# Spreading attention's reciprocals over features by DMA instead of by matmul, with a new order of the work around it

## The chip, the cores and the metric

The kernel runs on one core of one Trainium2 chip. The metric is device time in microseconds (us) of one execution. The kernel before took 1003.21 us (median of 4 runs, 1002.76 to 1003.95).

## The reference, cut to what matters

Linear attention over 8 batches of 8 heads (576 tokens, 64 features) is followed by a mixture of 8 experts. Only the attention's last division is concerned here:

```python
num = np.einsum('bhsf,bhfd->bhsd', q_p, kv)
den = np.einsum('bhsf,bhf->bhs', q_p, z)[..., None] + 1e-06
return (num / den).astype(np.float32)
```

There is one denominator for each head and token, and each divides 64 features. The expert layer after it takes the result with features on partitions, so every reciprocal must be present on the 64 partitions of its head.

## The kernel before

From about 24 to 184 us the kernel runs seven blocks, 0 to 6. Block j does the feed-forward of expert 0 for 512 tokens in 16 slots: slots 0 to 7 are the first matrix (`ffn1`), slots 8 to 15 the second (`ffn2`). The attention of batch b = j + 1 is scattered over these slots. Instructions keep the written order on TensorE (PE), VectorE (DVE) and ScalarE (ACT). The loads go through GpSimd's queue (POOL), the others through SyncE's (SP).

The reciprocals are split into two fp16 parts and spread over partitions by matmuls with a matrix of zeros and ones; ScalarE copies the result from PSUM, and VectorE multiplies:

```python
def attend(b, hk):
    parts = ((0, 2 * C3), (2 * C3, C))
    rb_ps = [ps_s.tile([P, 512], FP32, name="small_ps") for _ in parts]
    rb = rb_pool.tile([P, C * HP], FP32, name="rb")
    for i, (c0, c1) in enumerate(parts):
        for j in range(c0 // C3, c1 // C3):
            te.matmul(out=rb_ps[i][...], lhsT=spread[0:96, j, hk]..., rhs=hls[b][:], ...)
        se.copy(out=rb[:, c0 * HP : c1 * HP], in_=rb_ps[i][...])
    num_ps = [ps_s.tile([P, 512], FP32, name="small_ps") for _ in parts]
    for i, (c0, c1) in enumerate(parts):
        for hh in range(2):
            te.matmul(out=num_ps[i][...], lhsT=kvs[b][0][:, hk, hh, :], rhs=qTs[b, hk][...], ...)
        ve.tensor_tensor(out=xT[:, hk, ...], in0=num_ps[i][...], in1=rb[...], op=ALU.mult)

# schedule of a block j with batch b = j + 1 (cut)
at(j, 5, denominators, b)
for hk in range(HK):
    at(j, FT + 2 * hk, attend, b, hk)          # slots 8, 10, 12, 14
for half in range(2):
    at(j, 2 * half if j else 3, load, b + 1, half)
```

`small_ps` is a pool of four PSUM buffers. A half load is three DMAs (k, v and q of four heads), each 288 KB as written.

The softmax here doesn't subtract the row's maximum and nothing guards it: scores larger than these inputs give would overflow.

## Time and profile before

| what | number | where it is read |
|---|---|---|
| span of the profiled run | 1000.8 us | head of the page |
| one block, blocks 2 to 5 | 22.2 to 22.3 us | start of `ffn1` to start of the next, timeline of PE |
| PE busy in such a block | 21.9 to 22.0 us | windows |
| three spread matmuls | 0.34 us | timeline of PE |

The windows view of the kernel before, one line for each of blocks 2 to 5. The columns are the stretch, its length, the busy us and instruction count of each engine, the granted clock of PE, the DMA share and GB/s.

```profile
73.37:95.56 22.19, 21.87 (x244) 11.66 (x241) 17.33 (x37) 14.34 (x33) 4.30 (x6) 1.00 0.57 82
95.56:117.85 22.29, 21.97 (x247) 11.76 (x245) 17.33 (x37) 14.34 (x33) 4.29 (x6) 1.00 0.58 81
117.85:140.04 22.19, 21.87 (x243) 11.67 (x241) 17.34 (x37) 14.34 (x33) 2.15 (x3) 1.00 0.46 68
140.04:162.33 22.29, 21.97 (x247) 11.78 (x245) 17.34 (x37) 14.34 (x33) 0.00 (x0) 1.00 0.01 2
```

PE is idle for 0.3 us a block, the other engines for 4.9 us and more. Time can be saved only by taking work or waits from PE. The timeline of PE in the kernel before shows both (start, us, what; the bracket is the idle time before it and what ended it):

```profile
86.30 0.41 PE L100 MATMUL small_ps<-hl,acc_hi 96*128 96x192 f16 x3
86.64 0.44 PE L100 MATMUL small_ps<-q_pT,kv_sb 128*64 128x384 f16 x4
...
100.25 0.50 PE L100 MATMUL small_ps<-ident,q_p 128*128 128x128 f16 x6 [0.26 <-ACT kv_sb L100]
```

The three spread matmuls of one attend hold PE from 86.30 to 86.64. Four attends make 1.36 us a batch.

### The profile page before, as it was taken

The numbers are of one execution on the slowest core, as the hardware profiler recorded it, in microseconds if no ns is written. First come the engines' busy times: TensorE is split into PE (matmuls) and PEld (weight loads), VectorE is DVE, ScalarE is ACT, GpSimd is POOL, SyncE is SP. The second block draws the span as 40 slices with busy tenths as digits, with TensorE's granted clock in tenths as the row PEclk, the third lists the DMA queues.
The fourth block names the chain that finished last, engine by engine and source line by source line (L and its number), as shares of the span: only waits on it lengthen the run. The fifth ranks groups of instructions, "written<-read, shape, count | busy, mean of one in ns | idle before, by whom it ended". The sixth has DMA issues, their size and how long they took to land.

```text
span 1000.8 us, 20629 instructions
## 1 busy us (share of the span) xinstructions
PE 981.3 (98%) x8062; PEld 689.3 (69%) x8062; DVE 829.2 (83%) x1862; ACT 574.7 (57%) x1284; POOL 60.3 (6%) x82
## 2 busy tenths in 40 slices
PE   7999999989999999999999999999999999999997
PEld 6455555446777777777777777777777777777775
DVE  5888777588989888888879878988789888988886
ACT  5766666447777555555555555555555555555551
POOL 6412200001000000000000000000000000000001
PEclk9999999999999999999999999999999999999999
DMA  9966610534002331034013320043113400104535
GB/s 165 206 92 87 87 23 1 105 70 82 33 25 51 65 66 48 26 76 80 25 48 67 60 55 26 25 90 66 41 33 67 90 25 25 48 25 111 130 89 124
DMA packets 51922, 66.50 MB, mean 66 GB/s; under 512 B 4848, under 2 KB 43760, under 8 KB 51824
## 3 DMA queue, kind: packets, MB, share of 16 engines
q0 software_dynamic: 27232, 30.94, 20.0%
q1 hardware_dynamic: 24352, 33.98, 12.4%
q8 instruction: 63, 1.03, 0.4%
q10 hardware_dynamic: 240, 0.26, 0.1%
q14 instruction: 35, 0.29, 0.1%
HBM read 83.12 MB, written 12.98 MB: 96 GB/s over the span
## 4 chain that ended last, share of the span: by engine, by line
PE 72%; issue 21%; DVE 4%; ACT 1%; DMA 1%; POOL 1%; POOLq 0%; ACTq 0%; DVEq 0%
PE rows_ps L100 25%; PE h_ps L100 21%; PE copied_ps L100 8%; PE p_ps L100 8%; PE y_ps L100 5%; PE small_ps L100 5%; DVE k_p L100 1%; DMA v_ld<-in_v_dram 1%; DVE q_pT L100 1%; DVE q_p L100 0%; DVE den L100 0%; DVE xT L100 0%; DVE acc_lo L100 0%; DVE P_tok L100 0%; DVE v_aug_240 L100 0%
## 5 line engine op out<-in xcount | busy, mean ns | idle before, releaser
L762 DVE SCALAR_TENSOR_TENSOR acc_lo<-rows_ps,P_tok,acc_lo 128x512 f32<-128x512 f32 (+1 forms) x322 | 203.1, 639 | 74.8 <-PE rows_ps L100 74.7
L100 PEld LDWEIGHTS <-H 128*128 128x128 f16 x2080 | 203.0, 98 | 83.1 <-issue 1.2
L100 PEld LDWEIGHTS <-w1e 128*128 128x128 f16 x1632 | 155.9, 98 | 59.2 <-issue 4.9
L100 PE MATMUL h_ps<-xT,w1e 128*128 128x384 f16 (+1 forms) x616 | 152.9, 350 | 0.0
L730 ACT ACTIVATE H<-h_ps 128x384 f16<-128x384 f32 x144 | 70.6, 490 | 95.1 <-PE h_ps L100 95.1
L100 PE MATMUL rows_ps<-w2e,H 128*128 128x256 f16 (+1 forms) x568 | 91.2, 285 | 0.0
L711 ACT COPY copied_ps<-h_ps 128x384 f32<-128x384 f32 x144 | 67.5, 469 | 35.3 <-PE h_ps L100 35.3
L721 ACT ACTIVATE H<-copied_ps 128x384 f16<-128x384 f32 x144 | 70.8, 492 | 20.4 <-PE copied_ps L100 20.4
L100 PE MATMUL copied_ps<-xT,w1e 128*128 128x384 f16 x336 | 82.1, 326 | 0.0
L100 PE MATMUL copied_ps<-w2e,H 128*128 128x256 f16 x504 | 75.6, 272 | 0.0
L762 DVE SCALAR_TENSOR_TENSOR acc_lo<-copied_ps,P_tok,acc_lo 128x256 f32<-128x256 f32 x126 | 60.0, 476 | 0.6 <-PE copied_ps L100 0.2
L762 DVE SCALAR_TENSOR_TENSOR acc_hi<-rows_ps,P_tok,acc_hi 128x512 f32<-128x512 f32 (+1 forms) x56 | 41.3, 737 | 20.4 <-PE rows_ps L100 19.6
L777 DVE TENSOR_TENSOR H<-H 128x512 f16<-128x512 f16 x125 | 52.6, 421 | 2.6
L100 PE MATMUL y_ps<-w2e,hT 128*128 128x512 f16 x224 | 54.7, 380 | 0.0
L804 ACT COPY copied_ps<-rows_ps 128x256 f32<-128x256 f32 x111 | 39.7, 357 | 17.6 <-PE rows_ps L100 17.6
L100 ACT ACTIVATE hT<-h_ps 128x512 f16<-128x512 f32 x54 | 32.3, 600 | 17.0 <-PE h_ps L100 16.6
L100 DVE TENSOR_TENSOR xT<-small_ps,rb 128x384 f16<-128x384 f32 x64 | 26.2, 451 | 16.6 <-ACT rb L100 16.5
L118 POOL DMA_DIRECT2D w1e<-in_moe_w_dram x11 | 8.3, 763 | 509.0 <-DVE T_3_5030 L670 92.4
L100 PEld LDWEIGHTS <-hT 128*128 128x128 f16 x224 | 19.5, 98 | 25.0 <-issue 5.8
L100 ACT COPY rb<-small_ps 128x384 f32<-128x384 f32 x64 | 22.4, 402 | 22.7 <-PE small_ps L100 22.6
L100 DVE TENSOR_SCALAR q_pT<-small_ps 128x384 f16<-128x384 f32 x46 | 25.0, 552 | 9.3 <-PE small_ps L100 8.7
L100 ACT ACTIVATE H<-h_ps 128x384 f16<-128x384 f32 (+1 forms) x40 | 21.3, 532 | 15.4 <-PE h_ps L100 14.7
(2459 smaller groups left out, 2065.8 us busy)
## 6 DMA issues: line engine op xcount, KB each, us to landing
out_dram<-acc_lo SPq DMA_DIRECT2D x62, 128.0 KB, 2.4
w1e<-in_moe_w_dram POOLq DMA_DIRECT2D x7, 1024.0 KB, 8.9
w2e<-in_moe_w_dram POOLq DMA_DIRECT2D x7, 1024.0 KB, 9.5
k_ld<-in_k_dram POOLq DMA_DIRECT2D x16, 288.0 KB, 6.4
v_ld<-in_v_dram POOLq DMA_DIRECT2D x16, 288.0 KB, 7.3
q_ld<-in_q_dram POOLq DMA_DIRECT2D x16, 288.0 KB, 6.8
w1e<-in_moe_w_dram POOLq DMA_DIRECT2D x4, 256.0 KB, 10.4
w2e<-in_moe_w_dram POOLq DMA_DIRECT2D x4, 256.0 KB, 10.9
```

Source lines behind the costliest of these rows:

```text
L100: i = getattr(self.engine, name)(*args, **kwargs)
L118: nc.gpsimd.dma_start(out=w[0][:, :, f0:f1], in_=view[:, :, f0:f1])
L711: se.copy(out=Y[:, 0:TU], in_=X[:, 0:TU])
L721: se.activation(out=h11, in_=Y[:, 0:TU], func=AF.Relu)
L730: se.activation(out=h12, in_=X[:, 0:TU], func=AF.Relu)
L762: ve.scalar_tensor_tensor(out=a, in0=rows, scalar=P_tok[:, g, self.e : self.e + 1], in1=a, op0=ALU.mult, op1=ALU.add,)
L777: i = (nc.gpsimd if self.last else ve).tensor_tensor(out=out_, in0=in0, in1=in1, op=op)
L804: se.copy(out=self.W, in_=self.U)
```

## The change

For batches 3 to 7 the reciprocals go to DRAM in one store and come back in eight reads, each of which repeats rows over 64 partitions. Spread matmuls and PSUM copies of these batches go. To give the DMAs time, the denominators move to slot 4 (from block 3 on; block 2 keeps slot 5), the attends to slots 12 to 15, and much of the next batch's work comes a block earlier. Turns (transposes of q) come one a slot and more of them on ScalarE; y copies go to ScalarE. The loads are written in slots 13 and 15, behind the reads. `v_augs` moves into a part of the accumulator that is not in use yet, to make room for four `rb` buffers.

```diff
-            if g % 2 == 0:
+            if g % 2 == 0 or TCH // P <= g < (B - 1) * TCH // P:
                 se.copy(out=acc(g), in_=y_ps)
@@ denominators
             ve.reciprocal(out=den[:], in_=den[:])
+            if b >= 3:
+                r = dram.tile([96, C3 * HP], FP32, name="r")
+                nc.sync.dma_start(out=r[:], in_=den[:])
+                for hk in range(HK):
+                    rb = rb_pool.tile([P, C * HP], FP32, name="rb")
+                    for hh in range(2):
+                        h = 2 * hk + hh
+                        nc.sync.dma_start(
+                            out=rb[hh * HP : (hh + 1) * HP, :].rearrange("p (j s) -> p j s", j=3),
+                            in_=r[:].rearrange("(j r) s -> r j s", r=32)[h : h + 1].to_broadcast(
+                                [HP, 3, C3 * HP]
+                            ),
+                        )
+                    rbs[b, hk] = rb
+                return
@@ schedule (cut)
-                at(j, 5, denominators, b)
+                at(j, 5 if j <= 2 else 4, denominators, b)
                 for hk in range(HK):
-                    at(j, FT + 2 * hk, attend, b, hk)
+                    at(j, 8 + 2 * hk if j == 1 else 12 + hk, attend, b, hk)
...
+                for i, (hk, k_) in enumerate(turns[:8]):
+                    at(j, 8 + i, turn, b + 1, hk, k_, k_ != 1)
+                at(j, 10, sums, b + 1, 0)
+            if 1 <= j and b + 2 < B:
+                for half in range(2):
+                    at(j, 13 + 2 * half, load, b + 2, half)
```

More of the change, by code (lines that the diff above doesn't have):

```diff
@@ L179 @@
         kv_pool = p1.enter_context(tc.tile_pool(name="kv_pool", bufs=2))
-        rb_pool = p1.enter_context(tc.tile_pool(name="rb_pool", bufs=2))
+        rb_pool = p1.enter_context(tc.tile_pool(name="rb_pool", bufs=4))
         ps_y = p1.enter_context(tc.tile_pool(name="ps_y", bufs=2, space=bass.MemoryType.PSUM))
@@ L287 @@
         ve.tensor_copy(out=wg[:], in_=wg_ld[:])
-        kps, qps, qTs, kvs, hls = {}, {}, {}, {}, {}
-        v_augs = [cs_pool.tile([P, C, D + 2], F16, name=f"v_aug{i}") for i in range(4)]
+        kps, qps, qTs, kvs, hls, rbs = {}, {}, {}, {}, {}, {}
+        lent = acc_lo[:, G_LO - 4 : G_LO, :].rearrange("p g d -> p (g d)").bitcast(F16)
+        VA = C * (D + 2)
+        v_augs = [
+            lent[:, i * VA : (i + 1) * VA].rearrange("p (c d) -> p c d", d=D + 2)
+            for i in range(4)
+        ]
         for t in v_augs:
@@ L396, in denominators @@
             ve.reciprocal(out=den[:], in_=den[:])
+            if b >= 3:
[6 more added lines that the diff above has]
+                        nc.sync.dma_start(
+                            out=rb[hh * HP : (hh + 1) * HP, :].rearrange(
+                                "p (j s) -> p j s", j=3
+                            ),
+                            in_=r[:].rearrange("(j r) s -> r j s", r=32)[h : h + 1].to_broadcast(
+                                [HP, 3, C3 * HP]
+                            ),
+                        )
+                    rbs[b, hk] = rb
+                return
             hi = kv_pool.tile([96, C3 * HP], F16, name="hi")
@@ L408, in attend @@
             parts = ((0, 2 * C3), (2 * C3, C))
-            rb_ps = [ps_s.tile([P, 512], FP32, name="small_ps") for _ in parts]
-            rb = rb_pool.tile([P, C * HP], FP32, name="rb")
+            rb = rbs.pop((b, hk), None)
+            rb_ps = [ps_s.tile([P, 512], FP32, name="small_ps") for _ in parts if rb is None]
+            by_dma = rb is not None
+            if not by_dma:
+                rb = rb_pool.tile([P, C * HP], FP32, name="rb")
             for i, (c0, c1) in enumerate(parts):
+                if by_dma:
+                    break
                 for j in range(c0 // C3, c1 // C3):
@@ L546 @@
             elif b < B:
-                at(j, 0, prep_q, b, 3)
-                at(j, 1, prep_kv, b, 3)
-                at(j, 1, sums, b, 0)
-                at(j, 3, sums, b, 1)
-                for i, (hk, k_) in enumerate(turns[2:]):
-                    at(j, i // 2, turn, b, hk, k_)
-                at(j, 5, denominators, b)
+                if j <= 2:
+                    at(j, 0, prep_q, b, 3)
+                    at(j, 1, prep_kv, b, 3)
+                    at(j, 1, sums, b, 0)
+                    at(j, 3, sums, b, 1)
+                    for i, (hk, k_) in enumerate(turns[2:]):
+                        at(j, i // 2, turn, b, hk, k_, k_ != 1)
+                else:
+                    at(j, 0, sums, b, 1)
+                    for i, (hk, k_) in enumerate(turns[8:]):
+                        at(j, i, turn, b, hk, k_, k_ != 1)
+                at(j, 5 if j <= 2 else 4, denominators, b)
                 for hk in range(HK):
-                    at(j, FT + 2 * hk, attend, b, hk)
+                    at(j, 8 + 2 * hk if j == 1 else 12 + hk, attend, b, hk)
             if j:
                 at(j, 6, gates, j)
-            if b + 1 < B:
+            if j <= 1:
                 for half in range(2):
@@ L564 @@
                     at(j, NS - 1, turn, b + 1, hk, k_)
+            elif b + 1 < B:
+                for slot, fn, hk in (
+                    (4, prep_k, 0), (5, prep_q, 0), (6, prep_kv, 0), (6, prep_k, 1),
+                    (7, prep_q, 1), (8, prep_kv, 1), (9, prep_k, 2), (10, prep_q, 2),
+                    (11, prep_kv, 2), (11, prep_k, 3), (13, prep_kv, 3), (15, prep_q, 3),
+                ):
+                    at(j, slot, fn, b + 1, hk)
+                for i, (hk, k_) in enumerate(turns[:8]):
[4 more added lines that the diff above has]
+                    at(j, 13 + 2 * half, load, b + 2, half)
         y_pss = {}
```

## The prediction

> **What bounds the kernel now.** The change touches only the first 190 us: eight blocks in which TensorE interleaves the expert-0 feed-forward of block j with the attention of batch j+1. In the timeline, blocks 2 to 6 repeat every 22.2 to 22.3 us; the windows view gives TensorE 21.9 to 22.0 us busy in each, VectorE 17.3, ScalarE 14.3, DMA share 0.56 while batches load, 0.03 later. The granted clock is 1.00. The chain of waits is PE there too. So only instructions taken from TensorE, or its one regular wait (0.26 us a block, for the kv_sb copy on ScalarE), can shorten a block.
>
> **Removed, for batches 3 to 7 (blocks 2 to 6).** Twelve 96x192 broadcast matmuls a batch. The PE timeline shows three starting 0.34 us ahead of the next kind, so 4 x 0.34 = 1.36 us a batch, all on the critical path: 6.8 us in five batches. On ScalarE eight rb copies (4 x (0.478 + 0.325) = 3.2 us a batch), on VectorE hi and hl (0.67 us). Both are off the path. Spreading turns over slots may also remove part of the 0.26 us wait, at most 1.5 us in all.
>
> **Added.** One store of 96x192 and eight broadcast reads a batch on the SP queue: 1536 pieces of 768 B, 1.18 MB. From the hardware queue's packets in the DMA view of the first 200 us (960 packets, 37 ns each on one engine) I estimate 4.3 us for the reads alone, after two fixed latencies. The Trainium skill ("DMA: Bandwidth & Descriptors", Anatomy of one DMA) gives about 2.0 us fixed, mostly the write receipt; this trace's 128 KB stores land in 2.4 us, which agrees. The denominators end near 6.4 us into a block, the reciprocal near 8.4, the store near 10.6, the reads between 13 and 17 us. The attends, now last, need them at about 15.6 to 19.8 us. That fits unless the loads collide: their order waits for buffers, which come free near slot 7, not for the slot where they are written, so one half batch (about 4.4 us of DMA at 200 GB/s) competes with the reads. I expect the reads late by 0 to 1 us.
>
> **Moved.** y copies go to ScalarE, more turns too: VectorE falls to about 14.2 us a block, ScalarE stays near 13. But attends sit in slots 12 to 15: VectorE then has four times 0.90 us of products, one k_p and v copy (1.2) and a turn (0.55) before the last product, 5.4 us after slot 12's numerators, and the next block's first ffn1 needs that product 0.64 us after it starts. I estimate a new PE wait of 0.3 to 0.6 us a block at the boundary.
>
> **Sum.** 1.36 + about 0.2 - about 0.5 = about 1.1 us a block, five blocks: 5.5 us; everything after is relative to that, and moves unchanged. Predicted 997.2 us, 80% range 993.0 to 1002.0. Faster by over 2% 0.01, within 2% 0.97, slower by over 2% 0.02.
>
> **Right or wrong in the profile.** Right: blocks 3 to 6 of 20.8 to 21.4 us; 60 fewer matmuls small_ps<-hl; idle of VectorE before xT put down to the rb DMA of under 1 us; a PE wait on VectorE's xT at block starts; phase two unchanged. Wrong: blocks still of 22 us with PE waiting for xT or for small_ps, or blocks under 20.6 us with no wait at the boundary.
>
> **What would make it wrong.** The 64-fold read of the same rows being much slower than 37 ns a piece; loads arriving late for prep because the SP reads take the DMA engines; four small_ps buffers running out when VectorE waits for a late rb; VectorE's order delaying k_p for the sums.

## The result, and the profile after

The changed kernel took 1009.91 us (median of 4 runs, 1009.32 to 1012.43). The ratio to the kernel before is 1.0071 (95% interval 1.0053 to 1.0089): 0.7% slower. Ratios here are the mean time of one kernel's runs over that of the other's of the same rounds, so not quite the ratio of the medians quoted.

Windows of the changed kernel, blocks 2 to 6:

```profile
74.87:103.34 28.47, 24.05 (x285) 12.73 (x283) 16.53 (x37) 16.26 (x37) 5.08 (x9) 0.94 0.75 128
103.34:130.68 27.34, 22.56 (x236) 11.41 (x233) 14.67 (x32) 13.97 (x30) 4.97 (x7) 0.94 0.63 114
130.68:151.27 20.59, 20.59 (x231) 10.64 (x230) 14.19 (x31) 13.73 (x29) 0.71 (x1) 1.00 0.52 103
151.27:171.92 20.65, 20.65 (x235) 10.71 (x233) 14.30 (x31) 13.88 (x30) 0.00 (x0) 1.00 0.26 62
171.92:190.34 18.42, 18.42 (x171) 8.62 (x168) 6.44 (x14) 8.62 (x19) 0.00 (x0) 1.00 0.30 69
```

Blocks 4 and 5 gain 1.6 us each, more than predicted. Blocks 2 and 3 take 28.5 and 27.3 us. Block 6 is short because part of its work was moved to block 2. Everything from block 7 on runs as before, 6.85 us later (its gate matmuls start at 191.98 instead of 185.14).

The timeline of PE in the changed kernel shows where blocks 2 and 3 stop:

```profile
97.13 0.37 PE L100 MATMUL small_ps<-q_pT,kv_sb 128*64 128x192 f16 x2 [3.11 <-DVE xT L100]
...
97.73 1.91 PE L100 MATMUL y_ps<-w2e,hT 128*128 128x512 f16 x4
...
101.42 0.27 PE L100 MATMUL small_ps<-q_pT,kv_sb 128*64 128x192 f16 x2 [1.31 <-DVE xT L100]
...
121.36 0.27 PE L100 MATMUL small_ps<-q_pT,kv_sb 128*64 128x192 f16 x2 [0.57 <-DVE xT L100]
...
127.32 0.37 PE L100 MATMUL small_ps<-q_pT,kv_sb 128*64 128x192 f16 x2 [4.22 <-DVE xT L100]
...
127.92 1.91 PE L100 MATMUL y_ps<-w2e,hT 128*128 128x512 f16 x4
```

PE needs a `small_ps` buffer for the next numerators and finds all four taken, because VectorE has not worked off the earlier ones: its products, and behind them the copy of a turn. VectorE in turn waits for the reads (its timeline, same kernel):

```profile
96.52 0.82 DVE L100 TENSOR_TENSOR xT<-small_ps,rb 128x384 f16<-128x384 f32 x2 [4.75 <-DMA rb<-r]
...
100.81 0.82 DVE L100 TENSOR_TENSOR xT<-small_ps,rb 128x384 f16<-128x384 f32 x2 [3.00 <-DMA rb<-r]
...
126.71 0.82 DVE L100 TENSOR_TENSOR xT<-small_ps,rb 128x384 f16<-128x384 f32 x2 [4.67 <-DMA rb<-r]
```

The stop is paid twice. After a long one, four `y_ps` matmuls take 1.91 us instead of 1.03. The Trainium skill ("TensorE: Matmul & The Clock Gate", Part 1) says that the clock halves after an idle window of about 3.4 us; the trace agrees in kind: the windows view gives a granted clock of 0.50 from 96.60 to 100.00 us and from 127.32 to 130.73 us, so 0.94 over each of these blocks, and 1.00 in the others.

Why the reads are late shows in GpSimd's queue. The first half load of batch 6 is written in slot 13 of block 3 but issued at 88.6 us, in block 2, as soon as its buffers are free; batch 7's goes in block 3 in the same way. The changed kernel's timeline of POOL, and below it that of SP's queue:

```profile
88.62 0.72 POOL L192 DMA_DIRECT2D q_ld<-in_q_dram  x1 [9.30 <-DVE q_p L100]
89.33 0.72 POOL L192 DMA_DIRECT2D k_ld<-in_k_dram  x1
90.04 0.73 POOL L192 DMA_DIRECT2D v_ld<-in_v_dram  x1
...
114.43 0.71 POOL L192 DMA_DIRECT2D q_ld<-in_q_dram  x1 [8.64 <-DVE q_p L100]
```

```profile
86.04 0.34 SPq L406 DMA_DIRECT2D r<-den  x1
87.75 8.50 SPq L411 DMA_DIRECT2D rb<-r  x8
111.86 0.32 SPq L406 DMA_DIRECT2D r<-den  x1
113.47 7.24 SPq L411 DMA_DIRECT2D rb<-r  x8
139.23 0.31 SPq L406 DMA_DIRECT2D r<-den  x1
140.81 5.15 SPq L411 DMA_DIRECT2D rb<-r  x8
```

In blocks 2 and 3 the loads go out while the reads do. In block 4 (139 to 146 us) no load does, and there is no stop. The DMA view of the changed kernel, first for 84 to 104 us (block 2), then for 138 to 152 us (block 4); a queue's line ends with the share of 16 engines' time in that stretch, an issue's with the median us to landing:

```profile
q1 hardware_dynamic: 1776, 1.25, 29.7%
q0 software_dynamic: 839, 0.91, 28.6%
...
rb<-r SPq DMA_DIRECT2D x8, 144.0 KB, 7.9
```

```profile
q1 hardware_dynamic: 1776, 1.25, 38.4%
...
rb<-r SPq DMA_DIRECT2D x8, 144.0 KB, 4.4
```

Alone, store and reads need 0.384 x 14 = 5.4 us of all 16 DMA engines. The three loads need 0.286 x 20 = 5.7 us. Together that is over 11 us, and the time from the store's landing to the last attend is shorter than that where nothing stops: 9.9 us in block 4 (140.81 to 150.72).

The same views bear on a rival, that the packets themselves become slower beside the loads. Share times stretch times 16 engines over the number of packets gives, for store and reads, 54 ns a packet in block 2, 48 in block 3 (24.1% of 110 to 132 us) and 48 in block 4. So the packets took about a tenth longer at most; what grew is their waiting.

### The profile page after: what moved, and what is told of

It is laid out like the page before. It is cut to its first block, busy times and chain, and to the rows that moved or that the text cites. A ratio compares the mean times of both kernels' runs of the same rounds, so it can differ in the third digit from the quotient of the medians.

```text
span 1007.5 us, 20503 instructions
## 1 busy us (share of the span) xinstructions
PE 979.1 (97%) x8002; PEld 685.8 (68%) x8002; DVE 812.3 (81%) x1828; ACT 573.3 (57%) x1268; POOL 60.3 (6%) x82
## 4 chain that ended last, share of the span: by engine, by line
issue 75%; PE 15%; DMA 3%; DVE 3%; POOL 2%; SPq 1%; ACT 0%; POOLq 0%; DVEq 0%; ACTq 0%
PE h_ps L100 5%; PE small_ps L100 5%; PE y_ps L100 3%; DMA rb<-r 3%; PE rows_ps L100 1%; DVE den L100 1%; DMA k_ld<-in_k_dram 1%; SPq L411 1%; POOL w2e L124 0%; PE copied_ps L100 0%; DVE xT L100 0%; POOL w1e L118 0%; DVE k_p L100 0%; DMA r<-den 0%; POOL acc_lo L973 0%
## 5 line engine op out<-in xcount | busy, mean ns | idle before, releaser
L100 PE MATMUL y_ps<-w2e,hT 128*128 128x512 f16 x224 | 58.1, 389 | 0.0
L809 DVE SCALAR_TENSOR_TENSOR acc_hi<-rows_ps,P_tok,acc_hi 128x512 f32<-128x512 f32 (+1 forms) x56 | 41.3, 738 | 20.5 <-PE rows_ps L100 19.7
L100 ACT ACTIVATE q_pT<-small_ps 128x384 f16<-128x384 f32 x62 | 29.7, 494 | 23.5 <-PE small_ps L100 23.2
L100 PEld LDWEIGHTS <-q_p 128*128 128x128 f16 x288 | 20.9, 101 | 15.3 <-issue 5.4
L100 DVE TENSOR_SCALAR q_pT<-small_ps 128x384 f16<-128x384 f32 x34 | 18.4, 553 | 15.5 <-PE small_ps L100 15.5
```

The costliest lines, as they stand in the source:

```text
L100: i = getattr(self.engine, name)(*args, **kwargs)
L809: ve.scalar_tensor_tensor(out=a, in0=rows, scalar=P_tok[:, g, self.e : self.e + 1], in1=a, op0=ALU.mult, op1=ALU.add,)
```

## The experiments

Theory 1 was that the early loads collide with the reads on the DMA engines. Theory 2: the chain of store and eight issues is too long for slot 12 whatever else runs. Theory 3: the new schedule itself overloads VectorE or the four `small_ps` buffers.

### Loads of batches 6 and 7 held to the end of a block (hold67)

```diff
+        HELD = {(6, 0): (3, 3), (6, 1): (3, 3), (7, 0): (4, 3), (7, 1): (4, 3)}
         def load(b, half, names="qkv"):
...
-                nc.gpsimd.dma_start(
+                i = nc.gpsimd.dma_start(...)
+                held_by = HELD.get((b, half))
+                if held_by is not None:   # wait for the last product of that attend(batch, hk)
+                    tc.add_manual_dep(i.ins, attended[held_by].ins.name, <Sync, DATA>, ...)
```

> The changed kernel, with one thing added: the loads of batches 6 and 7 wait for the last product of batch 3's and batch 4's attends (end of blocks 2 and 3), so they can't share the DMA engines with the spread reads of blocks 2 and 3. Theory 1 (the loads collide with the reads): VectorE's waits for rb fall from 23.2 us to under 4 us, PE's waits of 3.1, 1.3, 0.6 and 4.2 us in blocks 2 and 3 go, and with them the slow clock after them; block 3 takes about 20.7 us as blocks 4 and 5 did; time 996 to 1000 us. Theory 2 (the chain of store and eight issues of 0.6 us is too long for slot 12, whatever else runs): the waits stay near 5 us a block, time 1007 to 1010 us. Theory 3 (the new schedule overloads VectorE or small_ps at the end of a block): the waits stay too.

Measured: 1002.68 us, ratio 0.9999 (0.9984 to 1.0014). That is about 7 us better than the changed kernel but misses the 996 to 1000 expected. Block 2 is freed (22.41 us, no idle PE). Blocks 3 and 4 take 25.10 and 23.26 us, with PE waits of 2.39 and 2.46 us for VectorE's product. The timeline of SP in this run shows why:

```profile
106.94 0.32 SPq L417 DMA_DIRECT2D r<-den  x1
112.56 5.15 SPq L422 DMA_DIRECT2D rb<-r  x8
...
154.87 0.31 SPq L417 DMA_DIRECT2D r<-den  x1
156.46 5.17 SPq L422 DMA_DIRECT2D rb<-r  x8
```

Held to the end of block 2, six loads are issued at once, from 99.6 us, and keep the DMA engines busy until about 111.5 us. The store of block 3 is issued into that at 106.94 us and takes 5.6 us to land instead of 1.6 (block 4's takes 4.9). So not only the reads but the 72 KB store before them must have the DMA engines free. I had seen that the loads would just about end when the reads start, and had left the store out.

### Only batch 6 held (hold6)

The edit is the same with the two entries of batch 6 alone.

> The same hold for batch 6 alone. Theory 1: block 2 loses its stall, block 3 keeps one of 5 to 7 us, because the first half of batch 7 is still issued in the middle of block 3's reads; time 1002 to 1005 us. Theories 2 and 3: both blocks stay stalled, or neither changes; time near 1010 us.

Measured: 1001.46 us, ratio 0.9987 (0.9972 to 1.0002); slightly below the range. Block 2 takes 22.94 us; block 3 still takes 26.76, with one PE wait of 4.19 us; block 4 takes 20.55. Windows of this run, blocks 2 to 4:

```profile
73.59:96.53 22.94, 22.63 (x285) 12.39 (x283) 16.60 (x36) 16.37 (x37) 2.17 (x4) 1.00 0.68 121
96.53:123.29 26.76, 22.37 (x236) 11.15 (x233) 14.57 (x32) 13.64 (x29) 7.88 (x11) 0.94 0.88 150
123.29:143.84 20.55, 20.55 (x231) 10.60 (x229) 14.30 (x31) 13.87 (x30) 0.71 (x1) 1.00 0.54 103
```

Moving one batch's loads takes the stall out of one block. Theories 2 and 3 cannot say that. (Some of block 3's stall is again the store, which took 5.5 us.)

### All reciprocals spread by matmul, new schedule kept (matmul_spread)

```diff
-            if b >= 3:
+            if b >= B:
```

> The changed kernel with all reciprocals spread by matmul as before; schedule, turns, y copies and load order of the change are kept. Theory 1: no wait for rb, no stall; each of blocks 2 to 6 pays 1.36 us of matmuls again, so 6.8 us more than hold67: 1003 to 1006 us, and faster than the changed kernel by 4 to 7 us. Theory 3: the schedule's stalls stay without any DMA, time near 1010 us or above.

Measured: 1006.81 us, ratio 1.0038 (1.0023 to 1.0053), just outside my range. There is no large stall, so theory 3 does not explain blocks 2 and 3. But block 3 takes 23.29 us, 2.6 more than block 5 of the changed kernel, where 1.36 was expected. PE waits for ScalarE at the end of each block (its timeline in this run):

```profile
117.99 0.33 PE L100 MATMUL small_ps<-ident,q_p 128*128 128x128 f16 x3 [0.44 <-ACT rb L100]
...
122.21 0.33 PE L100 MATMUL small_ps<-ident,q_p 128*128 128x128 f16 x3 [0.44 <-ACT rb L100]
```

The new order, with four attends in four slots and turns between them, is made for reciprocals that need no PSUM. With the matmul spread it is worse than the old order by about 1 us a block.

### Larger pieces, loads not held (big_pieces)

```diff
-                r = dram.tile([96, C3 * HP], FP32, name="r")
-                nc.sync.dma_start(out=r[:], in_=den[:])
+                r = dram.tile([32, 3 * C3 * HP], FP32, name="r")
+                for j in range(3):
+                    nc.sync.dma_start(out=r[:, j * C3 * HP : (j + 1) * C3 * HP],
+                                      in_=den[32 * j : 32 * j + 32, :])
...
-                            out=rb[...].rearrange("p (j s) -> p j s", j=3),
-                            in_=r[:].rearrange("(j r) s -> r j s", r=32)[h : h + 1].to_broadcast(...),
+                            out=rb[hh * HP : (hh + 1) * HP, :],
+                            in_=r[h : h + 1, :].to_broadcast([HP, 3 * C3 * HP]),
```

> The changed kernel, loads not held, with the reciprocals stored head by head (three stores of 32x192), so that each partition reads one piece of 2304 B instead of three of 768 B: a third of the pieces, the same bytes. If the time of the reads goes by pieces, their DMA work falls from about 5.4 us a batch to 2 to 3 us and the stalls of blocks 2 and 3 shrink to 2 to 3 us each: 1001 to 1005 us. If it goes by bytes, the stalls stay within 1 us of the changed kernel's: 1008 to 1011 us.

Measured: 1001.31 us (five runs, 1000.43 to 1005.56), ratio 0.9978 (0.9962 to 0.9995). The time is in the range of "by pieces", but the profile does not say so plainly. In an undisturbed block (block 5), a third of the pieces lowers the work of store and reads from about 5.2 us (25.8% of a 20 us stretch in the changed kernel) to 3.9 us (19.7% of 20 us), and the median landing of a read from 4.3 to 3.1 us. So, if the two costs simply add, most of the time goes by bytes. The profiled run was the slowest of the five: its block 2 took 29.1 us, its block 3 23.6 us. How the others split is not known, so this run shows that less DMA work helps, not by how much in which block.

### Loads in the gaps between reads and the next store (gap_loads)

```diff
+        HELD = {(6, 0): (3, 1), (6, 1): (4, 1), (7, 0): (4, 1), (7, 1): (5, 1)}
```

> The changed kernel with the four half loads of batches 6 and 7 put into the gaps between one batch's reads and the next batch's store: batch 6's first half after batch 3's second attend, its second half and batch 7's first half after batch 4's second attend, batch 7's last half after batch 5's. In the run with both loads held to the end of a block the store of 72 KB took 5.5 us to land instead of 1.6, because the loads were still in flight when it was issued. If sharing of the DMA engines is the whole cause (theory 1, completed by that), stores land in about 1.6 us and reads in 4 to 5 us in every block, blocks 2 to 5 take about 22.4, 20.7, 20.7 and 20.7 us, PE's waits for rb vanish, time 995 to 998 us. If there is a further cost of the spread by DMA, blocks 3 and 4 stay over 21.5 us and the time over 999 us.

Measured: 996.44 us (five runs, 994.74 to 998.96), ratio to the kernel before 0.9939 (0.9926 to 0.9953). Windows of this run, blocks 2 to 5:

```profile
73.65:96.00 22.35, 22.35 (x286) 12.16 (x284) 16.58 (x37) 16.23 (x37) 3.86 (x7) 1.00 0.69 125
96.00:116.65 20.65, 20.65 (x235) 10.69 (x233) 14.41 (x31) 13.82 (x30) 2.50 (x4) 1.00 0.52 105
116.65:137.21 20.56, 20.56 (x232) 10.60 (x229) 14.40 (x31) 13.87 (x30) 4.31 (x7) 1.00 0.82 150
137.21:157.86 20.65, 20.65 (x235) 10.68 (x233) 14.30 (x31) 13.88 (x30) 0.12 (x1) 1.00 0.51 103
```

PE is never idle, the clock stays at 1.00, and the store lands in 1.6 to 2.15 us. Nothing was removed: the same loads run at other times. Block 2 is 28.47 - 22.35 = 6.1 us shorter and block 3 27.34 - 20.65 = 6.7 us shorter than in the changed kernel. That is 12.8 of the 14.5 us between the two profiled runs (1007.5 and 993.0); another 1.2 us is an earlier start of the first `ffn1` (24.64 against 25.85). In both together PE was idle for 4.42 + 4.78 = 9.2 us, and its busy time was 1.70 + 1.91 = 3.6 us longer (slow clock). The profiled run is the fastest of the five; the slowest (998.96 us) shows a mean clock of 0.994 against 0.996, so a stop may have come back in it, but it was not profiled.

### One and three loads put back beside the reads (dose1, dose3)

These are a positive control. Loads that nobody reads are added to the kernel with gaps, in block 5 alone; the output stays correct.

```diff
+        def extra(after_b, names):
+            for name in names:
+                x = ld.tile([P, 2, C, D], F16, name=f"{name}_ld")
+                i = nc.gpsimd.dma_start(out=x[:]..., in_=view[:, 0:2])
+                tc.add_manual_dep(i.ins, recips[after_b].ins.name, <Sync, DATA>, ...)
...
+        at(5, 5, extra, 6, "q")       # dose1; "qkv" in dose3
```

> A positive control on the run with gaps alone (996.4 us, block 5 of 20.65 us without a PE wait): one load of 288 KB that nobody reads is issued in block 5 when the reciprocals of batch 6 are done, beside their store and reads. Its DMA work is about 1.9 us (a third of the 5.7 us that three took). Theory 1: the reads of block 5 land 1 to 3 us later, block 5 grows by 0 to 2 us, all other blocks stay; time 996 to 999 us. If loads beside the reads are harmless, nothing changes.

> The same with three such loads (5.7 us of DMA work) in block 5 alone. Theory 1: block 5 shows what blocks 2 and 3 of the changed kernel showed, PE waits for VectorE's product of 3 to 5 us and slow matmuls behind them; block 5 takes 25 to 28 us, all other blocks 20.6 us as before; time 1001 to 1004 us.

Measured: 997.10 us (ratio 0.9944, 0.9928 to 0.9961), in its range, and 1004.52 us (ratio 1.0016, 0.9999 to 1.0032), just above it. Block 5 in the windows of dose1 and then of dose3, to be read against the 20.65 us above:

```profile
138.54:159.73 21.19, 20.89 (x235) 10.85 (x233) 14.31 (x31) 13.90 (x30) 0.84 (x2) 1.00 0.66 114
```

```profile
139.68:165.76 26.08, 22.59 (x236) 11.41 (x233) 14.59 (x32) 13.99 (x30) 2.88 (x5) 0.91 0.68 118
```

None, one and three loads give 20.65, 21.19 and 26.08 us. The reads' median landing goes from 4.4 to 6.3 to 8.5 us. One load fits into the slack almost entirely; three bring back the stall of blocks 2 and 3, slow clock included. In dose3, blocks 3 and 4 took 21.4 and 21.2 us, not 20.6, with waits of 0.4 to 0.55 us for the product: the slack there is small.

### Gaps with larger pieces (gap_big)

The gaps, and the layout of big_pieces with one store: `nc.sync.dma_start(out=r[:].rearrange("r (j s) -> j r s", j=3), in_=den[:])`.

> The same gaps, and the reciprocals stored head by head with one store, so that a read is 64 pieces of 2304 B. In the earlier run with big pieces the reads took 3.9 instead of 5.2 us of DMA work and landed in 3.1 instead of 4.3 us, but their issue stayed near 5 us. With the gaps no read is on the path any more, so the time should be that of the run with gaps alone, within 1.5 us.

Measured: 995.64 us (five runs, 995.21 to 996.32), ratio 0.9926 (0.9914 to 0.9939). It is as fast as the gaps alone, as expected, with less scatter (1.1 us against 4.2 between extreme runs). This is the fastest kernel of the study, 0.7% under the kernel before.

### Batch 2 by DMA as well (gap_b2)

```diff
-            if b >= 3:
+            if b >= 2:
-                    at(j, 8 + 2 * hk if j == 1 else 12 + hk, attend, b, hk)
+                    at(j, 12 + hk, attend, b, hk)
```

(with the gaps and the entry `(5, 0): (2, 1)`)

> The gaps, and batch 2 spread by DMA too (its attends move to slots 12 to 15 of block 1, batch 5's first half load waits for its second attend). Block 1 then loses its twelve matmuls, 1.36 us, and takes 20.3 to 20.6 us instead of 21.8: 1.0 to 1.6 us less than the gaps alone, if the reads of block 1 meet no load; if they do, block 1 stalls by 3 us or more.

Measured: 1001.07 us, ratio 0.9979 (0.9966 to 0.9991): a miss, 4.6 us worse than the gaps alone. Block 1 takes 23.06 us instead of 21.78, with PE waits of 0.67, 0.25 and 0.86 us for VectorE's products; its store took 2.6 us, with batch 4's second half load, issued until 57 us, not long before it. In block 6 of the profiled run, which took 20.24 us instead of 18.43, the store took 3.7 us although no load was in flight, and PE waited 1.16 us there. What delayed that store was not found, so that part of the loss stays open. It suggests how thin the slack is with 768 B pieces.

### The y copies alone (before_ycopy, gap_ydve)

First the kernel before with nothing but the first hunk of the diff; then, later, the gaps with that hunk undone.

> The kernel before with the y copies of blocks 1 to 6 all on ScalarE and nothing else of the change. PE is busy 21.9 of 22.2 us in a block, so moving work between two engines off the path should give nothing: within 1.5 us of before. If the y copies are what frees the schedule, the 0.26 us wait a block goes: 1 to 2 us faster.

> The gaps, with the y copies back where they were: every second one on VectorE. The run of the kernel before with only the y copies changed was 3.3 us faster than before, against my expectation, by 0.65 us a block. If VectorE's backlog costs as much in the new schedule (1.37 us of copies come back to it in each block, and attends last), blocks 3 to 5 grow from 20.6 to 21.2 us or more and the time to 999 to 1003 us. If the new schedule has slack for it, the time stays within 1.5 us of 996.4.

Measured: before_ycopy 999.54 us, ratio 0.9965 (0.9952 to 0.9977), against my expectation; gap_ydve 996.51 us, ratio 0.9935 (0.9920 to 0.9950), no different from gap_loads. Block 3 of before_ycopy in the windows:

```profile
96.06:117.71 21.65, 21.65 (x247) 11.73 (x245) 16.07 (x35) 15.31 (x36) 4.28 (x6) 1.00 0.56 84
```

The block went from 22.29 to 21.65 us with the same number of matmuls, and PE has no idle time left. In the old order VectorE came into each block with a backlog; `zsel`, `kv_sb` and a turn's `small_ps` came late by way of it, which is the 0.26 us wait shown before and a stretched group of turns beside it. Taking 1.3 us of y copies from VectorE removes that. In the new order the k and q preparation lies elsewhere, and putting the copies back costs nothing that was measured. So the gains do not add up: of the 6.4 us between the kernel before and gap_loads, one line in the old order would have given 3.3.

## Why the prediction was wrong

Predicted: 997.2 us (993.0 to 1002.0). Measured: 1009.91. The kernel with loads in the gaps takes 996.44, so the other terms were near enough in sum (6.4 us gained where 5.5 were expected), though not one by one, and one was not.

- "I expect the reads late by 0 to 1 us." This step failed. The collision itself was foreseen, and so was its cause: loads follow their buffers, not the slot where they are written. Its size was wrong. The DMA work was 5.4 us for store and reads and 5.7 us for a half load, against 4.3 (reads alone) and 4.4 estimated. Above all I took the reads as served in the order in which they were needed. With loads in flight, the median read landed after 7.9 to 9.5 us and one after 12.1. Even the first attend's product in block 2 started only at 96.52, 8.8 us after the first read was issued, and the second attend was held up as hard as any: VectorE waited 4.75 + 3.00 us in block 2 and 2.32 + 4.67 us in block 3.
- What a late read costs was left out. VectorE's wait uses up the four `small_ps` buffers within 2 us (numerators at 92.16, PE stopped from 94.02), so it becomes PE's wait (9.2 us in both blocks), and then the clock halves (3.6 us). My list of what could go wrong had the buffers in it, without a number; it did not have the clock.
- "1.36 us a batch", plus 0.2 from the turns: right in sum. Undisturbed blocks went from 22.2 or 22.3 to 20.6 us, 1.6 us. The runs don't split it as I did: the y copies alone were worth 0.65 us a block in the old order, and from there to the gaps a block went from 21.65 to 20.65 us, 1.0 and not 1.36. That the sum came out is in part luck.
- "A new PE wait of 0.3 to 0.6 us a block at the boundary": wrong for blocks 3 to 6, which show none with loads in the gaps; the 0.5 us a block was subtracted for nothing. Only the start of block 7 has it (0.55 us in the changed kernel).
- "Everything after is relative to that, and moves unchanged": right. The shift of 6.85 us at block 7's gates is the shift of the end (1007.5 - 1000.8 = 6.7 us).
- About 2 us of that difference is probably no effect of the change: the first `ffn1` matmul started at 25.85 instead of 23.90 us. In the other profiles it started between 24.6 and 26.5 us, in before_ycopy at 25.04 with the code before it unchanged. That looks like scatter of the start; only two profiles show it for the old code.

## What to carry to other kernels

Writing a DMA later in the program does not hold it back: it goes when its queue reaches it and its buffers are free. If it must stay clear of a DMA that somebody waits for, give it a dependence on an instruction that marks the end of the critical stretch, and count the small store at the head of the chain as part of that stretch. Before moving work from a matmul to DMA, add up the DMA time of everything that can be in flight between the issue and the use, and ask what stops when it comes late: here a pool of four PSUM buffers turned VectorE's wait into TensorE's, with a slow clock on top.

## What the Trainium skill lacked or had wrong

- "DMA: Bandwidth & Descriptors", Issuing engines are not separate DMA queues: it says that DMAs of all issuing engines interleave on the same 16 DMA engines. The runs agree and add the size: beside three loads of 288 KB, the median landing of a 144 KB read rose from 4.4 us to 7.9 and 9.5.
- The same section calls the issue time "usually small relative to the DMA itself". Here one read with 64-fold repetition took about 0.6 us to issue on SP, and eight took 5.15 us undisturbed, as long as their work on the DMA engines (5.4 us with the store). Beside loads the eight took 8.50 us.
- The same page, Anatomy of one DMA, gives about 2.0 us fixed plus the bytes at 436 GB/s, for a DMA on GpSimd's path. The store here, on SyncE's queue, moves 72 KB; it landed in 1.6 us on free engines and in 4.9 to 5.6 us behind six loads. The page has no number for a small DMA beside large ones.
- "TensorE: Matmul & The Clock Gate", Part 1, gives an idle window of about 3.4 us, free-running. Waits of 3.11 us and 2.39 us were followed by matmuls at half speed here, and one of 1.93 us (big_pieces, clock 0.50 from 125.60 to 129.01 us), while one of 2.46 us was not (hold67, clock 1.00 over that block). A gap well under 3.4 us can already cost the clock. An estimate of what decides, from these traces: the slow stretches are 3.41 us long (hold67, from 117.81) or twice that (dose3, from 161.20). In the 3.41 us before one began, PE was idle for 1.93 us (hold67, big_pieces) and 1.83 us (dose3); the 2.46 us wait, counted in the same steps, falls into two of them, with 1.4 and 1.1 us. These traces fit a rule in which the idle time within one step decides, at some value between 1.4 and 1.8 us; no run was made to test it.
- No page that I read has a size for what taking copies from an engine that is 78% busy gives in blocks in which TensorE is 98% busy: the y copies gave 0.65 us a block, by the account above through late buffers.
